# One second mix over the first two tiles, and the first sums split between VectorE and Pool

## The chip, the cores and the metric

The kernel runs on one core of a Trainium2 chip. The metric is the device time of one execution in microseconds (us); before the change it is 791.39 us, the median of three runs (790.71 to 791.91).

## The reference

Three stages follow each other on two batches of 4160 positions with 192 channels. The first is a windowed sum with 8 heads, the second and third are channel mixes with 1024 hidden channels.

```python
w = softmax(weight_gen, axis=-1)                     # 8 heads x 7 positions
out = np.einsum('bshk,bskhg->bshg', w, x_unf)        # 7 positions of x, weighted and summed
# first mix
xk = mu_k * x + (1.0 - mu_k) * x_prev                # xr the same with mu_r
k = np.maximum(xk @ w_k, 0.0)
x = sigmoid(xr @ w_r) * (k * k @ w_v)
# second mix
h = np.maximum(x @ w_in, 0.0)
conv_out = sum(conv_w[k] * hp[:, k:k + S, :] for k in range(3))   # three neighbouring positions
out = h * sigmoid(conv_out) @ w_out
```

## The kernel before, in words

The positions are cut into ten tiles (`SIZES`: 256, 248, seven of 472, 352). For each tile and batch the work has these steps.

- **Sums** (`attention`): for each slot (a set of 128 positions, one per partition) a `token` multiplies the 7 rows by the weights (`prod`, 1344 columns) and folds them in three additions (576, 384 and 192 columns) into `tok`. There are 2 slots in each of the first two tiles, 4 in the others. All sums are done by Pool, with one scratch tile `prod`.
- **Mixing in** (`mixing`): TensorE turns `tok` into channel-major form in a `pa` bank (matmuls with `ident`); u = 0 holds the first 128 channels of batch 0, u = 1 those of batch 1, and u = 2 the last 64 of both. ScalarE and VectorE form the mixed inputs. They are split into a high and a low part (`xA`, and for u = 2 `rm` and `mk`, which DMAs copy into `xB`).
- **First mix** (`moe1`, `gate_r`, `mix_out`): 8 groups per tile and batch. Each has five matmuls into `pa`, Relu, Square and a copy on ScalarE, a subtraction on VectorE (high and low part `s`), and five matmuls into `am` and `ar`. Two gates of five matmuls each complete it, and `mix_out` writes the result to `x2`.
- **Second mix** (`moe2`, `store`): again 8 groups per tile and batch: five matmuls into `pc`, four operations on ScalarE and four on VectorE (`h`, the taps, Sigmoid, `g`), and five matmuls into `bm` and `br`. `carry` copies the last two columns of a tile in front of the next.

The weights arrive as 64-bit floats and are turned into a high and a low 32-bit part by `narrow` and `split` (VectorE, ScalarE and the tile `stage`). This goes on beside the first tiles. The softmax weights `sw` of tiles 0, 1 and 2 are made separately; those of tiles 3 to 9 are one load, worked on tile by tile.

The order on each engine is not written by hand. Each closure enters a plan with a due time (`at`), and `Program.schedule` simulates the engines with the costs of `cost` and always takes the ready operation that is due first. The result is a fixed list of instructions for each engine. An engine runs its list in order and waits where an input is missing. All instructions are therefore on line 167 in the profile.

Of the kernel before, what the change touches and what calls it, by code (L numbers as in the profile page):

```python
# [12 lines left out]
AX = mybir.AxisListType  # L13

NB, SEQ, DM, NH, KS, DFF = 2, 4160, 192, 8, 7, 1024
SIZES = [256, 248] + [472] * 7 + [352]
NTILE = len(SIZES)
STARTS = [sum(SIZES[:i]) for i in range(NTILE)]
NMAX = max(SIZES)

PART = [128] * NTILE
SLOTS = [2, 2] + [4] * 7 + [3]
# [2 lines left out]
WIN = KS * DM  # L25
NF = DFF // 128
LAG = 10


def f(ap):  # L30
# [3 lines left out]
class Program:  # L34
# [37 lines left out]
    def cost(self, eng, method, out, ins, pointer):  # L72

        n = self.count(out)
        src = [self.space(x) for x in ins]
        if method == "dma_start":
            return 0.6, 0.0
        if eng == "PE":
            busy = max(n * 0.00045 + 0.002, 0.109)
            return busy, busy + 0.24  # L80
        if eng == "ACT":
            near = bool(src) and src[0] == "PSUM"
            p = 0.1 if pointer else 0.0
            return (0.06 if near else 0.09) + p + n / 1200, (0.2 if near else 0.24) + p + n / 1200
        if eng == "DVE":
            if method == "tensor_reduce":
                n = self.count(ins[0])
            if method == "reciprocal":
                return 0.07 + n / 160, 0.2 + n / 160
            if method in ("tensor_scalar", "tensor_copy", "memset") and "PSUM" not in src:  # L90
                return 0.07 + n / 1920, 0.2 + n / 1920
            stt = method == "scalar_tensor_tensor"
            return (0.13 if stt else 0.07) + n / 960, (0.26 if stt else 0.2) + n / 960
        if eng == "POOL":
            busy = 0.1 + (n / 455 if method == "tensor_tensor" else n / 270)
            return busy, busy + 0.12
        return 0.6, 0.6

    def schedule(self):
# [41 lines left out]
        start = [0.0] * n  # L141
        for _ in range(n):
            t, eng = min((max(free[e], min(ready[i] for i in w)), e) for e, w in open_.items() if w)
            i = min((i for i in open_[eng] if ready[i] <= t), key=lambda i: (self.ops[i][4], i))
# [12 lines left out]
            if self.ops[i][1] == "dma_start":  # L157
                wires[eng] = max(wires[eng], t + dur[i] + 0.6) + moved[i]
                end = wires[eng] + 0.8
            for j in succ[i]:  # L160
                ready[j] = max(ready[j], t + dur[i] if eng == "PE" == self.ops[j][0] else end)
                left[j] -= 1
                if not left[j]:
                    open_[self.ops[j][0]].append(j)
# [17 lines left out]
def conv_moe_kernel(ctx: ExitStack, tc: tile.TileContext, xp, wg_first, wg_rest, mus, w_k, w_v, w_r, w_in, conv_w, w_out, out):  # L182
# [11 lines left out]
    def ring(name, n, shape, dtype=F32):  # L194
        return Ring([new(f"{name}{j}", shape, dtype) for j in range(n)])
# [48 lines left out]
    sm = []  # L244
# [126 lines left out]
    def softmax(j, a, b, eng, times, bank):  # L371
# [18 lines left out]

        for t, fn in zip(times, (lambda: fold(m, ALU.max), lambda: each(m, ALU.subtract), s3,
                                 lambda: fold(z, ALU.add), s5, lambda: each(m, ALU.mult))):
            at(t, fn)

# [6 lines left out]
    def attention(i, b, t_load, t, dt_, eng, hold=(0.0, 0.0)):  # L401
# [7 lines left out]
        def token(l):  # L409
            if i not in tok_t:  # L410
                tok_t[i] = tok_r()
            p = prod
            y = p.rearrange("p (k d) -> p k d", k=KS)
            w = sw[:, sum(slots[:i]) + b * L + l].unsqueeze(2).to_broadcast([128, KS, DM // NH, NH])
            eng.tensor_tensor(p.rearrange("p (k g h) -> p k g h", k=KS, h=NH),
# [159 lines left out]
    def carry(i, b, t):  # L575
        def go():
            if i == 0:
                POOL.memset(f(x2[b][:, :, 0:2]), 0.0)
            else:
                n = SIZES[i - 1]  # L580
                ACT.copy(x2[b][:, :, 0:2], f(x2[b][:, :, n:n + 2]))
            if i == NTILE - 1:
                n = SIZES[i]
                POOL.memset(f(x2[b][:, :, n + 2:n + 4]), 0.0)
        at(t, go)

    def mix_out(i, b, t):
        N = SIZES[i]
        X = x2[b]
        c = slice(2, N + 2)  # L590
        m, r = am_r.tiles[0], ar_r.tiles[0]

        def d0():
# [28 lines left out]

    def moe2(i, b, fi, t):
        last = i == NTILE - 1
        N = SIZES[i] + (2 if last else 0)
        X = x2[b]
        st = {}
        sl = slice(128 * fi, 128 * fi + 128)
# [50 lines left out]
        at(t + 2.75, go2)  # L679

    def store(i, b, t):
        N = SIZES[i]
        last = i == NTILE - 1
        a = 1 if i == 0 else 0
        n = N + (1 if last else 0)
        t0 = STARTS[i] - 1
        st = {}

        def e0():
# [22 lines left out]
    def identity():  # L712
# [12 lines left out]
    prepare((-99.75, -99.7, -99.4), [(-82, chunk_rem(w_k, wkB, True)), (-81, chunk_in(w_k, wkA, 0)),  # L725
                                     (-0.5, chunk_out(w_v, wv, 0)), (0.4, chunk_out(w_v, wv, 1)), (1.0, chunk_in(w_k, wkA, 1)),
                                     (1.4, chunk_out(w_v, wv, 2)), (2.4, chunk_out(w_v, wv, 3)), (3.4, chunk_r()),
                                     (4.4, chunk_rem(w_in, wiB, False)), (5.0, chunk_in(w_in, wiA, 0)), (6.0, chunk_out(w_out, wo, 0)),
                                     (6.4, chunk_conv()), (7.0, chunk_in(w_in, wiA, 1)), (8.0, chunk_out(w_out, wo, 1)),
                                     (9.0, chunk_out(w_out, wo, 2)), (10.0, chunk_out(w_out, wo, 3))])  # L730
    softmax_load(2, wg_rest[:, slots[1] * KH:(slots[1] + slots[2]) * KH], -99.3)
    softmax(2, 0, slots[2], POOL, (0.9, 0.91, 0.92, 0.93, 0.94, 0.95), None)
    softmax_load(3, wg_rest[:, (slots[1] + slots[2]) * KH:], 10.2, 40.0)
# [7 lines left out]
    for i in range(NTILE):  # L741
# [6 lines left out]
        for b in range(NB):  # L748
            t = T + 8 * b
            carry(i, b, t + 7)  # L750
            for k in range(2):
                gate_r(i, b, k, t + 5.12 + k)
            for fi in range(NF):
                moe1(i, b, fi, t + fi)
                moe2(i, b, fi, t + fi + LAG)
            mix_out(i, b, t + 8.52)
            store(i, b, t + LAG + 10.02)

    for t, _, fn, hold in sorted(plan, key=lambda e: e[:2]):
        prog.now, prog.hold = t, hold  # L760
# [66 lines left out]
```

## Time and profile before

| what | value |
|---|---|
| median of three runs | 791.39 us (790.71 to 791.91) |
| the profiled execution | 793.36 us, its span 791.6 us |
| TensorE busy | 697.2 us (88%), 3505 matmuls |
| ScalarE busy | 666.5 us (84%), 1441 instructions |
| VectorE busy | 631.4 us (80%), 1137 instructions |
| Pool busy | 506.2 us (64%), 368 instructions |
| mean granted TensorE clock | 0.973 |

The span is what the profiler records on the core; 1.8 us of the execution lie around it. The page divides the span into 40 slices. TensorE is idle in the first two, at 50 to 70% in the next five, at 90% or more from the eighth to the thirty-eighth, and lower in the last two. Pool is busy from the start to about 430 us.

### The profile page before, as it was taken

To read this page: it belongs to the slowest core of one execution; us is meant where nothing else is said; L and a number is where in the kernel's file an instruction comes from. 1 tells how busy PE (TensorE), PEld (TensorE's weight loads), DVE (VectorE), ACT (ScalarE), POOL (GpSimd) and SP (SyncE) were. 2 spreads that over 40 slices of the span, in tenths; PEclk is the share of its full clock that TensorE was granted. 3 is DMA by queue.
4 is the path that set the end of the run, shared out by engine and by line. 5 is a ranking of instruction groups with operands and counts; after the bars stand their busy time and mean duration, and the time that the engine had idled before them with its cause. 6 is when DMAs were issued, how large, how long until landed. Compare 5 with 4: busy or idle time off the path is not lost.

```text
span 791.6 us, 10781 instructions
## 1 busy us (share of the span) xinstructions
PE 697.2 (88%) x3505; PEld 607.3 (77%) x3505; DVE 631.4 (80%) x1137; ACT 666.5 (84%) x1441; POOL 506.2 (64%) x368
## 2 busy tenths in 40 slices
PE   0066776999999999999999999999999999999964
PEld 0054675898888888888888888888888888889843
DVE  5987977887878787878877887879787878788764
ACT  2467798998989899989898989989898989899854
POOL 5898888899999999999999789295401101000000
PEclk9997786999999999999999999999999999999998
DMA  7685010130130112112121211020002000100000
GB/s 202 194 277 174 13 51 11 58 103 10 61 99 19 51 69 59 59 51 91 28 69 51 68 46 58 7 68 1 20 12 56 20 1 21 35 19 1 20 14 14
DMA packets 19241, 45.09 MB, mean 57 GB/s; under 512 B 3057, under 2 KB 14705, under 8 KB 19057
## 3 DMA queue, kind: packets, MB, share of 16 engines
q1 hardware_dynamic: 19184, 44.41, 18.9%
q8 instruction: 27, 0.44, 0.2%
q14 instruction: 30, 0.24, 0.1%
HBM read 27.40 MB, written 6.39 MB: 43 GB/s over the span
## 4 chain that ended last, share of the span: by engine, by line
PE 68%; ACT 15%; DVE 13%; issue 2%; DMA 2%; SPq 0%; ACTq 0%; DVEq 0%
PE pa L167 21%; PE pc L167 16%; PE am L167 10%; PE bm L167 9%; PE ar L167 7%; PE br L167 5%; DVE pc L167 4%; ACT pa L167 2%; ACT pc L167 2%; DVE stage L167 2%; ACT h L167 2%; ACT g L167 2%; ACT L167 1%; DMA stage<-in_moe_w_k_dram 1%; DVE bm L167 1%
## 5 line engine op out<-in xcount | busy, mean ns | idle before, releaser
L167 DVE SCALAR_TENSOR_TENSOR pc<-h,cw,pc 128x472 f32<-128x472 f32 (+3 forms) x320 | 208.1, 650 | 39.5 <-ACT pc L167 36.7
L167 POOL TENSOR_TENSOR prod<-rows,sw 128x1344 f32<-128x1344 f32 x70 | 216.1, 3087 | 12.8 <-DMA rows<-in_x_dram 7.8
L167 ACT ACTIVATE pa<-pa 128x472 f32<-128x472 f32 (+3 forms) x320 | 160.8, 505 | 39.1 <-PE pa L167 35.2
L167 POOL TENSOR_TENSOR prod<-prod 128x576 f32<-128x576 f32 (+1 forms) x140 | 171.0, 1221 | 8.6
L167 PE MATMUL bm<-g,wo 128*128 128x472 f32 (+3 forms) x480 | 148.7, 360 | 21.3 <-ACT g L167 21.1
L167 PE MATMUL am<-s,wv 128*128 128x472 f32 (+3 forms) x480 | 147.0, 367 | 7.1 <-ACT s L167 5.8
L167 DVE TENSOR_TENSOR pc<-h,pc 128x472 f32<-128x472 f32 (+3 forms) x160 | 94.7, 592 | 59.2 <-ACT pc L167 57.9
L167 PE MATMUL pa<-xA,wkA 128*128 128x472 f32 (+3 forms) x480 | 125.9, 368 | 7.5 <-DVE s L167 3.4
L167 PE MATMUL pc<-x,wiA 128*128 128x474 f32 (+3 forms) x480 | 121.6, 361 | 3.5 <-DVE g L167 3.5
L167 POOL TENSOR_TENSOR xA<-mk,xA 128x472 fp32r<-128x472 f32 (+2 forms) x36 | 40.4, 1128 | 123.1 <-ACT xA L167 96.6
L167 PE MATMUL ar<-s,wv 128*128 128x472 f32 (+3 forms) x320 | 112.6, 364 | 4.9 <-DVE x L167 3.3
L167 PEld LDWEIGHTS bm<-g,wo 128*128 128x128 f32 x480 | 88.3, 191 | 35.4 <-ACT g L167 26.0
L167 PE MATMUL br<-g,wo 128*128 128x472 f32 (+3 forms) x320 | 112.4, 355 | 1.4 <-DVE ob L167 1.4
L167 DVE TENSOR_TENSOR s<-pa,s 128x472 fp32r<-128x472 f32 (+3 forms) x160 | 93.7, 586 | 16.8 <-ACT s L167 15.8
L167 DVE TENSOR_TENSOR g<-pc,g 128x472 fp32r<-128x472 f32 (+3 forms) x160 | 93.8, 586 | 15.5 <-ACT g L167 14.0
L167 PEld LDWEIGHTS am<-s,wv 128*128 128x128 f32 x480 | 89.1, 197 | 21.4 <-ACT s L167 11.0
L167 PEld LDWEIGHTS pa<-xA,wkA 128*128 128x128 f32 x480 | 87.6, 199 | 19.9 <-DVE s L167 6.4
L167 ACT ACTIVATE pc<-h,cw 128x472 f32<-128x472 f32 (+3 forms) x160 | 99.7, 623 | 1.8
L167 PEld LDWEIGHTS pc<-x,wiA 128*128 128x128 f32 x480 | 85.7, 193 | 15.9 <-DVE g L167 5.8
L167 ACT ACTIVATE h<-pc 128x474 f32<-128x474 f32 (+3 forms) x160 | 84.4, 527 | 11.4 <-PE pc L167 8.3
L167 ACT ACTIVATE pc<-pc 128x472 f32<-128x472 f32 (+3 forms) x160 | 80.9, 506 | 14.0 <-DVE pc L167 13.0
L167 PE MATMUL pa<-xB,wkB 128*128 128x472 f32 (+3 forms) x320 | 89.8, 362 | 1.5 <-DMA xB<-mk 1.5
(105 smaller groups left out, 1066.4 us busy)
## 6 DMA issues: line engine op xcount, KB each, us to landing
rows<-in_x_dram SPq DMA_DIRECT2D x14, 960.0 KB, 4.5
xB<-rm SPq DMA_DIRECT2D x28, 118.0 KB, 2.3
xB<-mk SPq DMA_DIRECT2D x28, 118.0 KB, 2.3
out_dram<-om SPq DMA_DIRECT2D x14, 236.0 KB, 2.0
rows<-in_x_dram SPq DMA_DIRECT2D x4, 768.0 KB, 7.1
rows<-in_x_dram SPq DMA_DIRECT2D x2, 864.0 KB, 4.5
out_dram<-ob SPq DMA_DIRECT2D x14, 118.0 KB, 2.2
stage<-in_moe_w_v_dram SPq DMA_DIRECT2D x4, 384.0 KB, 3.9
```

Source lines behind the costliest of these rows:

```text
L167: getattr(self.real[eng], method)(*a, **k)
```

## The change

- The second tile gets 220 positions instead of 248, and the seven large ones 476 instead of 472.
- The second mix of tile 0 is no longer run by itself. Its input stays in `x2` in front of that of tile 1 (`OFFSET`), and one second mix of 476 columns (`UNIT`) follows once tile 1 has gone through the first mix. `carry`, `moe2` and `store` work on these units.
- VectorE does the sums of batch 0 of tile 0 with a scratch tile of its own (`prod0`, which lies in the second `tok` buffer). Pool does those of batch 1, with a hold of 16 us in the planner. The rows of tile 0 are loaded before the softmax weights.
- The softmax of tiles 3 to 9 takes its Exp as one instruction of 3024 columns. Its other steps, and the preparation of `w_in`, `w_out` and `conv_w`, have later due times.
- The planner knows other costs for Pool, and lets an engine wait up to 0.2 us for an operation that is due before -80.

```diff
-SIZES = [256, 248] + [472] * 7 + [352]
+SIZES = [256, 220] + [476] * 7 + [352]
+OFFSET = [0, SIZES[0]] + [0] * (NTILE - 2)
+UNIT = [None, SIZES[0] + SIZES[1]] + SIZES[2:]
+AHEAD = 0.2
...
-            busy = 0.1 + (n / 455 if method == "tensor_tensor" else n / 270)
-            return busy, busy + 0.12
+            busy = 0.15 + (n / 455 if method == "tensor_tensor" else n / 270)
+            return busy, busy + 0.1
...
+    prod0 = tok_r.tiles[1].rearrange("p a b -> p (a b)")[:, :WIN]
...
-            p = prod
+            p = prod0 if eng is DVE else prod
...
-    at(-100.5, consts)
+    at(-99.8, consts)
...
-    attention(0, 0, -99.9, -90, 0.1, POOL)
-    attention(0, 1, -99.6, -83.7, 0.1, POOL)
+    attention(0, 0, -100.1, -90, 0.1, DVE)
+    attention(0, 1, -99.6, -83.7, 0.1, POOL, (0.0, 16.0))
...
-        softmax(3, a, b, POOL, (16.5 + 0.3 * j, 16.6 + 0.3 * j, 19.5 + 0.1 * j, 20.5 + 0.5 * j, 20.6 + 0.5 * j, 24.9 + 16 * j), None)
+        softmax(3, a, b, POOL, (22 + 0.4 * j, 25 + 0.02 * j, None, 26.5 + 0.7 * j, 26.6 + 0.7 * j, 28.9 + 16 * j), None)
+    at(26, lambda: ACT.activation(sm[3][0], sm[3][0], ACTF.Exp))
...
-                moe2(i, b, fi, t + fi + LAG)
+                if i:
+                    moe2(i, b, fi, t + fi + LAG)
             mix_out(i, b, t + 8.52)
-            store(i, b, t + LAG + 10.02)
+            if i:
+                store(i, b, t + LAG + 10.02)
```

VectorE's list right behind the softmax of tile 0, before (the operations on `bm`, `pc0` and `stage` turn the weights `w_k` into 32-bit parts):

```order
L167 TENSOR_TENSOR sw_107<-sw_107,smz0_108 128x224
L167 TENSOR_SCALAR bm_117<-bm_117 128x512
L167 SCALAR_TENSOR_TENSOR bm_117<-stage_75,bm_117 128x512
L167 TENSOR_SCALAR pc0_113<-bm_117 128x512
L167 SCALAR_TENSOR_TENSOR stage_75<-stage_75,pc0_113 128x512
```

The same place now:

```order
L173 TENSOR_TENSOR sw_107<-sw_107,smz0_108 128x224
L173 TENSOR_TENSOR tok1_80<-rows0_76,sw_107 128x1344
L173 TENSOR_TENSOR tok1_80<-tok1_80 128x576
L173 TENSOR_TENSOR tok1_80<-tok1_80 128x384
L173 TENSOR_TENSOR tok0_79<-tok1_80 128x192
```

The four operations of a sum, twice, stand in front of the weights now (the second four read alike).

Pool's list where the sums of tile 1 begin (`rows0` again, into `tok1`), before:

```order
L167 TENSOR_TENSOR tok0_79<-prod_78 128x192
L167 TENSOR_TENSOR prod_78<-rows0_76,sw_107 128x1344
L167 MEMSET att0_81 128x1
L167 MEMSET att1_82 128x1
L167 TENSOR_TENSOR prod_78<-prod_78 128x576
```

The same place now:

```order
L173 TENSOR_TENSOR sw_107<-sw_107,smz2_110 128x448
L173 TENSOR_TENSOR sw_107<-sw_107,smz1_109 128x224
L173 MEMSET att0_81 128x1
L173 MEMSET att1_82 128x1
L173 TENSOR_TENSOR prod_78<-rows0_76,sw_107 128x1344
L173 TENSOR_TENSOR prod_78<-prod_78 128x576
```

The two small fills of `att` for u = 1 of tile 0 stood behind the first multiplication of tile 1, and stand ahead of it now.

ScalarE's list at the first Exp of tiles 3 to 9, before:

```order
L167 ACTIVATE pa0_111<-pa0_111 128x256 x2
L167 ACT_TABLE_LOAD
L167 ACTIVATE sw_107<-sw_107 128x448
L167 ACT_TABLE_LOAD
L167 ACTIVATE pc0_113<-pc0_113 128x256
```

The same place now:

```order
L173 ACTIVATE pa1_112<-pa1_112 128x220 x2
L173 ACT_TABLE_LOAD
L173 ACTIVATE sw_107<-sw_107 128x3024
L173 CAST rm00_85<-mk0_83 128x476
L173 ACT_TABLE_LOAD
```

Six further Exps with their table loads are gone, and the copy to `rm00` (tile 2, u = 2) stands behind the one that is left.

Pool's list ahead of this Exp, now (it ends the sums of tile 2, then subtracts the maxima of tiles 3 to 9):

```order
L173 TENSOR_TENSOR tok0_79<-prod_78 128x192
L173 TENSOR_TENSOR sw_107<-sw_107,stage_75 128x448 x6
L173 TENSOR_TENSOR sw_107<-sw_107,stage_75 128x336
L173 TENSOR_TENSOR xA00_87<-mk0_83,xA00_87 128x476
L173 TENSOR_TENSOR xA10_89<-mk1_84,xA10_89 128x476
```

The seven subtractions are behind all eight sums of tile 2 now, where six of them stood between the sums before.

## Rows read from the trace of the kernel before

**Rows 1.** By stretch: PE, PEld, DVE, ACT, POOL busy; granted clock, DMA share, GB/s.
```profile
20.00:40.00 20.00, 1.76 (x5) 0.76 (x5) 19.64 (x43) 8.07 (x20) 17.89 (x17) 1.00 0.69 194
40.00:140.00 100.00, 68.75 (x372) 61.57 (x372) 81.81 (x182) 77.65 (x195) 87.76 (x68) 0.81 0.32 103
140.00:160.00 20.00, 17.88 (x145) 16.85 (x143) 17.20 (x44) 19.12 (x59) 17.89 (x14) 1.00 0.17 60
160.00:200.00 40.00, 39.70 (x255) 36.23 (x256) 30.24 (x69) 35.92 (x96) 38.45 (x26) 1.00 0.19 55
```

**Rows 2.** Waits of 0 to 42 us: total, times, longest.
```profile
PE pa L167 <- POOL tok L167: 37.8, 4, 15.4
```

**Rows 3.** Timeline of Pool around 40 us: start, length, operation.
```profile
38.75 0.59 POOL L167 TENSOR_TENSOR tok<-prod 128x192 f32<-128x192 f32 x1
39.42 3.02 POOL L167 TENSOR_TENSOR prod<-rows,sw 128x1344 f32<-128x1344 f32 x1
...
45.75 3.04 POOL L167 TENSOR_TENSOR prod<-rows,sw 128x1344 f32<-128x1344 f32 x1
```

**Rows 4.** Chain that ended last, near 261 us: start, length, ten matmuls of 472 columns.
```profile
261.21 2.14 PE pa L167 x10
```

**Rows 5.** Busy groups by shape, ScalarE: total us, mean ns, idle before.
```profile
L167 ACT ACT_TABLE_LOAD x14 | 18.0, 1283 | 5.2 <-DMA sw<-in_first_dram 5.0
L167 ACT ACTIVATE sw<-sw 128x448 f32<-128x448 f32 x7 | 4.0, 578 | 0.2
```

**Rows 6.** Busy groups by shape, VectorE.
```profile
L167 DVE SCALAR_TENSOR_TENSOR pc<-h,cw,pc 128x472 f32<-128x472 f32 x224 | 158.8, 709 | 28.3 <-ACT pc L167 26.1
L167 DVE SCALAR_TENSOR_TENSOR pc<-h,cw,pc 128x256 f32<-128x256 f32 x32 | 15.4, 480 | 2.3 <-ACT pc L167 2.2
L167 DVE TENSOR_REDUCE stage<-sw 128x64 f32<-128x448 f32 x12 | 11.5, 977 | 5.5 <-ACT sw L167 5.5
L167 DVE RECIPROCAL stage<-stage 128x64 f32<-128x64 f32 x6 | 3.3, 550 | 0.4
L167 DVE TENSOR_SCALAR bm<-bm 128x512 uint32<-128x512 uint32 x4 | 2.8, 691 | 4.5 <-ACT bm L167 4.5
L167 DVE TENSOR_TENSOR sw<-sw,smz 128x224 f32<-128x224 f32 x2 | 0.8, 392 | 0.1
```

**Rows 7.** DMA issues of the first 1.9 us: KB each, us to landing.
```profile
rows<-in_x_dram SPq DMA_DIRECT2D x1, 768.0 KB, 7.3
sw<-in_first_dram SPq DMA_DIRECT2D x1, 112.0 KB, 3.7
```

**Rows 8.** Timeline of the loads: start and length of two issues on SP's queue.
```profile
3.98 0.55 SPq L167 DMA_DIRECT2D rows<-in_x_dram  x1
4.57 0.48 SPq L167 DMA_DIRECT2D sw<-in_rest_dram  x1
```

**Rows 9.** DMA issues of 3.9 to 4.7 us: KB each, us to landing.
```profile
rows<-in_x_dram SPq DMA_DIRECT2D x1, 768.0 KB, 10.6
...
sw<-in_rest_dram SPq DMA_DIRECT2D x1, 112.0 KB, 10.3
```

**Rows 10.** Timeline of VectorE: first and last operation of the softmax of tile 0.
```profile
4.92 0.55 DVE L167 TENSOR_REDUCE smz<-sw 128x32 f32<-128x224 f32 x1 [2.37 <-DMA sw<-in_first_dram]
...
7.89 0.39 DVE L167 TENSOR_TENSOR sw<-sw,smz 128x224 f32<-128x224 f32 x1
```

**Rows 11.** Timelines of Pool and VectorE near 120 us: one VectorE operation, twice.
```profile
118.67 3.06 POOL L167 TENSOR_TENSOR prod<-rows,sw 128x1344 f32<-128x1344 f32 x1
120.17 1.61 DVE L167 TENSOR_SCALAR stage<-stage 128x64 f32<-128x64 f32 x1
...
126.38 0.19 DVE L167 TENSOR_SCALAR stage<-stage 128x64 f32<-128x64 f32 x1
```

**Rows 12.** Busy groups by shape, Pool.
```profile
L167 POOL TENSOR_TENSOR sw<-sw,stage 128x448 f32<-128x448 f32 x12 | 13.6, 1140 | 5.6 <-DVE stage L167 3.4 <-ACT h L167 2.2
L167 POOL TENSOR_TENSOR xA<-mk,xA 128x248 fp32r<-128x248 f32 x4 | 2.8, 721 | 4.4 <-ACT xA L167 4.4
```

More of the change, by code (lines that the diff above doesn't have):

```diff
@@ L143, in schedule @@
             t, eng = min((max(free[e], min(ready[i] for i in w)), e) for e, w in open_.items() if w)
-            i = min((i for i in open_[eng] if ready[i] <= t), key=lambda i: (self.ops[i][4], i))
+            i = min((i for i in open_[eng] if ready[i] <= t + (AHEAD if self.ops[i][4] < -80 else 0.0)), key=lambda i: (self.ops[i][4], i))
+            t = max(t, ready[i])
             open_[eng].remove(i)
@@ L160, in schedule @@
             for j in succ[i]:
-                ready[j] = max(ready[j], t + dur[i] if eng == "PE" == self.ops[j][0] else end)
+                ready[j] = max(ready[j], t + dur[i] if eng in ("PE", "POOL") and eng == self.ops[j][0] else end)
                 left[j] -= 1
@@ L392, in softmax @@
                                  lambda: fold(z, ALU.add), s5, lambda: each(m, ALU.mult))):
-            at(t, fn)
+            if t is not None:
+                at(t, fn)
     rows_t, tok_t = {}, {}
@@ L578, in go @@
                 POOL.memset(f(x2[b][:, :, 0:2]), 0.0)
-            else:
-                n = SIZES[i - 1]
+            elif i > 1:
+                n = UNIT[i - 1]
                 ACT.copy(x2[b][:, :, 0:2], f(x2[b][:, :, n:n + 2]))
@@ L589, in mix_out @@
         X = x2[b]
-        c = slice(2, N + 2)
+        c = slice(OFFSET[i] + 2, OFFSET[i] + N + 2)
         m, r = am_r.tiles[0], ar_r.tiles[0]
@@ L624, in moe2 @@
         last = i == NTILE - 1
-        N = SIZES[i] + (2 if last else 0)
+        N = UNIT[i] + (2 if last else 0)
         X = x2[b]
@@ L681, in store @@
     def store(i, b, t):
-        N = SIZES[i]
+        N = UNIT[i]
         last = i == NTILE - 1
-        a = 1 if i == 0 else 0
+        a = 1 if i == 1 else 0
         n = N + (1 if last else 0)
-        t0 = STARTS[i] - 1
+        t0 = STARTS[i] - OFFSET[i] - 1
         st = {}
@@ L727, in conv_moe_kernel @@
                                      (1.4, chunk_out(w_v, wv, 2)), (2.4, chunk_out(w_v, wv, 3)), (3.4, chunk_r()),
-                                     (4.4, chunk_rem(w_in, wiB, False)), (5.0, chunk_in(w_in, wiA, 0)), (6.0, chunk_out(w_out, wo, 0)),
-                                     (6.4, chunk_conv()), (7.0, chunk_in(w_in, wiA, 1)), (8.0, chunk_out(w_out, wo, 1)),
-                                     (9.0, chunk_out(w_out, wo, 2)), (10.0, chunk_out(w_out, wo, 3))])
+                                     (6.0, chunk_rem(w_in, wiB, False)), (8.0, chunk_in(w_in, wiA, 0)), (10.0, chunk_out(w_out, wo, 0)),
+                                     (10.4, chunk_conv()), (12.0, chunk_in(w_in, wiA, 1)), (14.0, chunk_out(w_out, wo, 1)),
+                                     (16.0, chunk_out(w_out, wo, 2)), (18.0, chunk_out(w_out, wo, 3))])
     softmax_load(2, wg_rest[:, slots[1] * KH:(slots[1] + slots[2]) * KH], -99.3)
     softmax(2, 0, slots[2], POOL, (0.9, 0.91, 0.92, 0.93, 0.94, 0.95), None)
-    softmax_load(3, wg_rest[:, (slots[1] + slots[2]) * KH:], 10.2, 40.0)
+    softmax_load(3, wg_rest[:, (slots[1] + slots[2]) * KH:], 18.2, 50.0)
     for j in range(NTILE - 3):
         a, b = (sum(slots[3:3 + k]) for k in (j, j + 1))
-        softmax(3, a, b, POOL, (16.5 + 0.3 * j, 16.6 + 0.3 * j, 19.5 + 0.1 * j, 20.5 + 0.5 * j, 20.6 + 0.5 * j, 24.9 + 16 * j), None)
+        softmax(3, a, b, POOL, (22 + 0.4 * j, 25 + 0.02 * j, None, 26.5 + 0.7 * j, 26.6 + 0.7 * j, 28.9 + 16 * j), None)
+    at(26, lambda: ACT.activation(sm[3][0], sm[3][0], ACTF.Exp))
     mixing(0, 0, -88, 0.1)
```

## The prediction

> **What bounds the kernel now.** I read the busy time by stretch first, then the waits of the start, then timelines. From 160 us on, TensorE is busy 39.70 of 40 us [rows 1]: there only the amount of matmul work counts. Before that it is starved. To 40 us it waits 37.8 us for the sums of tile 0 [rows 2], the last of which Pool starts at 38.75 [rows 3]. From 40 to 140 us it executes 372 matmuls at a mean granted clock of 0.81, ScalarE and VectorE being busy 78 and 82 of 100 us [rows 1]. So the end moves by what TensorE has done by some time after the start, compared with before, minus any work added.
>
> I measure that in us of matmul work at the full rate. Ten matmuls of 472 columns take 2.14 us [rows 4], so one takes 0.214 us and a column 0.00045 us: 256 columns 0.116, 248 columns 0.113, 476 columns 0.216. By 140 us there are 377 matmuls, 372 from 40 us on and five before [rows 1], 12 of them turns of `tok` (0.07 each, my estimate for 128 columns with its overhead); that is 365 x 0.116 + 0.8 = 43.2 us. The 145 of the next stretch add 16.3: **59.5 us of work at 160 us** is the mark to beat. The 40 us behind it hold 38.2 us of work by the same count, a rate of 0.96.
>
> **Work added and removed on TensorE.** Seven tiles of 476: 7 x 340 matmuls x 4 columns x 0.00045 = +4.3 us. Tile 1's first mix, 180 matmuls with 28 columns less: -2.3. The second mix of both tiles, 160 matmuls of about 0.216 in place of 320 of 0.116 and 0.113 (their halos counted): 34.6 against 37.0, -2.4. Together about -0.4: the matmul work does not decide.
>
> **What the merge frees.** Two taps of 256 columns took 2 x 480 ns of VectorE, one of 472 takes 709 [rows 6]: 0.25 us saved for each pair. With four operations on each of two engines in 16 groups this is some 16 us on each (an estimate that gives all operations this saving). Ten table loads of 1.283 us [rows 5] go, 12.8 us of ScalarE. All of it lies between 80 and 160 us, where these engines set the pace, but in this kernel each engine runs a fixed list, so I follow the chain instead of adding up.
>
> **Start of the sums.** Before, `sw` lands 3.7 us and the rows 7.3 us after issue [rows 7], and the softmax ends 3.4 us after `sw` (4.92 to 8.28) [rows 10]. Now the rows are issued first. If `sw` still lands at 4.9, the softmax ends at 8.3, with the rows there at 8.0; if it lands just behind the rows, as a small load behind large rows does in [rows 8, 9] (4.57 + 10.3 against 3.98 + 10.6), it lands at 8.3 and the softmax ends at 11.7. The latter row is of the same pattern, but in a busier queue; I take 10.4 and keep both ends.
>
> A sum on VectorE: 392 ns at 224 columns and 691 at 512 [rows 6] give 0.16 us plus 1.04 ns a column, so 1344, 576, 384 and 192 columns take 1.56 + 0.76 + 0.56 + 0.36, with gaps 3.35 us, and two 6.7. Alone they would end at 17.1 (15.0 to 18.4).
>
> Pool's rows land at 3.98 + 10.6 = 14.6 [rows 8, 9], in the midst of this. Does VectorE wait for Pool there? The same VectorE operation took 0.19 us once and 1.61 at 120.17, where Pool's multiplication ran from 118.67 to 121.73: it ended right behind it [rows 11]. That operation has one input from SBUF; the two-input products of the softmax ran while Pool was idle, so no row shows a sum beside Pool. The Trainium skill (SBUF — State Buffer, section SBUF: two separate sides) says that a VectorE operation with two SBUF inputs, as a sum's all are, also shares a port pair with GpSimd, and that the later one blocks until the other instruction has ended. By that rule the two engines would alternate from 14.6 on; without it the sums would not touch each other. In numbers of rows: alternating with Pool's 3.0, 1.4, 1.0 and 0.6 us, VectorE ends at S = 20 to 27.4, depending on the start; not alternating, at 15.0 to 18.4. I take S = 22.5.
>
> **From S to the second tile.** Behind the sums VectorE has 24 operations up to the inputs of u = 2: twelve of 512 columns at 0.69 [rows 6], one of 384, six of 256 at 0.42 to 0.48, three reductions, two small; 14.2 us, less some 1 us of overlap: 13.2. Pool's two fills of `att` wait for the last of them, and the multiplication of tile 1 is behind the fills. So tile 1's sums start at S + 13.4 = 35.9 (39.42 before [rows 3]); before, those fills stood behind the multiplication.
>
> **Pool to the Exp.** Four sums of tile 1 at 6.33 us each (39.42 to 45.75 [rows 3], 6.4 with later ones), and one product of 1.14: 26.6. Eight sums of tile 2: 51.2. Six subtractions for tile 1's inputs at about 0.66 [rows 12], 4.0, and 1.5 for waits on ScalarE (4.4 us before in such places [rows 12]; here VectorE is ahead). Seven subtractions of maxima, 7.7 [rows 12]. Sum: 35.9 + 26.6 + 56.7 + 7.7 = 126.9.
>
> **The Exp and behind it.** ScalarE cannot pass its Exp. 448 columns take 0.578 us [rows 5], so 3024 at most 3.9, without the fixed part about 2.8: it ends at 129.8. Then VectorE takes seven reductions (0.977), seven additions (0.19 to 1.6 beside Pool) and seven reciprocals (0.55) [rows 6, 11], with a few groups in between: some 16 us, to T = S + 123.5 = 146. From there on nothing but matmul work is left in TensorE's way. It has then done tile 0's first mix (180 x 0.116), 172 matmuls of 220 columns (0.101), 50 of the merged second mix, five of tile 2 and 20 turns: 51.8 us. By 160 us that is 51.8 + 14 x 0.96 = 65.2, against 59.5: 5.7 of work, 5.9 us of time. I add 0.4 for the work, and take off 1.5 because TensorE idled in front of the softmax's end: the clock granted to the starved stretch is 0.81 [rows 1], between 1.2 and 2.4 GHz, and 15 to 20 matmuls at the lower level cost 1.5 to 4. **Gain: 4.8 us**, and the profiled execution of 793.36 would become 788.6. Against the median of 791.39, 0.25% below it, that is 786.6; I say **787**.
>
> **The rivals.**
> - *The engines do not hinder each other, and the softmax comes early*: then Pool's own end sets the turn (14.6 + 12.7 = 27.3, u = 2 ready at 30), tile 1 starts at 30.1, T = 140, work at 160 us 71.0: 11 us gained, **781**. For it: no row shows two-input waits. Against it: the one-input wait in [rows 11].
> - *The late start*: `sw` behind the rows and strict alternation, S = 27.4, T = 151, work at 160 us 60.5; gain within 0.5 us of nothing, **791**. All else in the change is then spent on the wait. This is also how it would read if the merge only removed work from engines with slack.
> - *VectorE becomes the bound* (the slower side). From S to T its list sums to 124 us, 111 with overlaps; my T allows it 12 us of idleness, 10%. It was idle 2% of 20 to 40 us but 18% of 40 to 140 us [rows 1]. With 18% again, T = S + 135.6 = 158, work at 160 us 53.8, 6 us lost: **796**. It decides from 13.5% of idleness on, where T reaches 150.7. For it: every weight is prepared later than before, by the 6.7 us of the sums and the wait, on the same engine that feeds each group. Against it: part of the 18% stood behind the seven Exps, 5.5 us in front of the reductions alone [rows 6], and one Exp is left.
>
> **How the numbers follow.** The forecast 0.40, no hindrance 0.17, the late start 0.16, VectorE as the bound 0.27. About 0.2%, 1.6 us, is what a measurement of this kernel can tell from no change. The first two are faster by more: 0.57. The third is the same: 0.16. The last is slower: 0.27. The forecast's own range is 783 to 790 (S from 20 to 25). With the bounds of the others to either side, 779 to 797 should hold the time 8 times in 10.
>
> **What the profile will show.** Right: VectorE's sums end near 22.5 with waits on Pool between them; Pool's first multiplication of tile 1 at 36; the long Exp at 127 to 130; TensorE nearly idle before it and full from 146 on; four table loads. Wrong would be: sums without stretched operations (then 781), a softmax end past 11 us (791), or VectorE with more than 13% of idle time between 23 and 146 us (796). If TensorE is not full from 150 to 200 us, or the large tiles run at less than 0.96, the step on the rest of the kernel failed.

## The result: 799.7 us, slower by 1.3%

The changed kernel takes **799.69 us** (median of four runs, 798.63 to 805.68) against 791.65 us for the kernel before in the same session (790.71 to 792.52). The ratio is 1.0132, with a 95% interval of 1.0098 to 1.0167. The profiled execution took 799.31 us, its span is 797.5 us; 791.6 us was the span of before. The forecast was 787, faster, with a range of 779 to 797. It was wrong in sign and in size. The profiled execution of before (793.36 us) lies 1.7 us above its median and this one 0.4 us below its own, so the two profiles show 5.9 of the 8.0 us.

The page gives the changed kernel's busy time, share and count for each engine:

```profile
PE 702.1 (88%) x3345; PEld 597.6 (75%) x3345; DVE 640.1 (80%) x1079; ACT 646.9 (81%) x1355; POOL 496.3 (62%) x360
```

ScalarE lost 20 us of work and Pool 10, VectorE gained 9, TensorE executes 160 matmuls less. None of that is where the time went. The stretches of the start show it (busy time by stretch, the columns as in [rows 1]):

```profile
20.00:40.00 20.00, 3.66 (x11) 2.19 (x11) 19.61 (x36) 7.50 (x18) 11.79 (x13) 1.00 0.47 138
40.00:140.00 100.00, 71.06 (x389) 61.19 (x390) 82.27 (x169) 68.26 (x181) 84.82 (x65) 0.89 0.40 129
140.00:160.00 20.00, 15.15 (x58) 12.77 (x59) 19.80 (x35) 11.31 (x26) 18.32 (x12) 0.63 0.18 41
160.00:200.00 40.00, 39.33 (x181) 32.92 (x180) 31.68 (x52) 34.83 (x70) 35.31 (x26) 1.00 0.16 58
...
22.50:153.60 131.10, 83.47 (x427) 70.55 (x428) 112.98 (x226) 81.35 (x211) 106.42 (x84) 0.86 0.41 126
...
149.00:154.60 5.60, 5.59 (x17) 4.97 (x18) 5.60 (x9) 2.49 (x6) 5.37 (x4) 0.50 0.00 0
```

From 140 to 160 us TensorE executes 58 matmuls (145 in [rows 1]) at a granted clock of 0.63, while VectorE is busy 19.80 of 20 us. In the line of 22.50 to 153.60, VectorE has 18.1 us of idle time between the end of its sums and the end of the long softmax, 13.8%.

To count TensorE's progress I add up, from the timeline, the columns of all matmuls that ended by a time, at 0.000453 us each. The totals are 647.7 us before and 647.6 now. By 140 us it is 42.5 before and 46.6 now, by 160 us 58.4 and **56.4**, by 250 us 143.6 and 142.8, by 700 us 582.7 and **577.7**. So the change is 2.0 us behind where TensorE fills up (0.8 at 250 us), and the large tiles lose 4.2 us more by 700 us. The last 100 us add 0.9, which makes the 5.9 us between the spans.

### The profile page after: what moved, and what is told of

Same layout as the page of the kernel before. It is cut to its first block, busy times and chain, and to the rows that moved or that the text cites. A ratio compares the mean times of both kernels' runs of the same rounds, so it can differ in the third digit from the quotient of the medians.

```text
span 797.5 us, 10286 instructions
## 1 busy us (share of the span) xinstructions
PE 702.1 (88%) x3345; PEld 597.6 (75%) x3345; DVE 640.1 (80%) x1079; ACT 646.9 (81%) x1355; POOL 496.3 (62%) x360
## 4 chain that ended last, share of the span: by engine, by line
PE 56%; ACT 11%; DVE 9%; issue 1%; POOL 1%; ACTq 0%; POOLq 0%
PE pa L173 17%; PE pc L173 14%; PE am L173 8%; PE bm L173 7%; PE ar L173 6%; PE br L173 5%; DVE pc L173 4%; ACT pc L173 2%; ACT h L173 2%; ACT pa L173 2%; ACT g L173 2%; DVE g L173 1%; DVE x L173 1%; ACT x L173 1%; DVE s L173 1%
## 5 line engine op out<-in xcount | busy, mean ns | idle before, releaser
L173 DVE SCALAR_TENSOR_TENSOR pc<-h,cw,pc 128x476 f32<-128x476 f32 (+1 forms) x288 | 201.2, 699 | 46.8 <-ACT pc L173 44.3
L173 ACT ACTIVATE pa<-pa 128x476 f32<-128x476 f32 (+3 forms) x320 | 160.4, 504 | 51.7 <-PE pa L173 47.9
L173 PE MATMUL am<-s,wv 128*128 128x476 f32 (+3 forms) x480 | 150.0, 369 | 15.4 <-ACT s L173 11.7
L173 PE MATMUL bm<-g,wo 128*128 128x476 f32 (+1 forms) x432 | 142.7, 379 | 19.0 <-ACT g L173 19.0
L173 PE MATMUL pa<-xA,wkA 128*128 128x476 f32 (+3 forms) x480 | 126.1, 371 | 17.9 <-ACT rm L173 9.7
L173 PE MATMUL pc<-x,wiA 128*128 128x478 f32 (+1 forms) x432 | 117.9, 380 | 0.0
L173 PE MATMUL ar<-s,wv 128*128 128x476 f32 (+3 forms) x320 | 113.6, 368 | 3.0 <-ACT x L173 2.9
L173 PE MATMUL br<-g,wo 128*128 128x476 f32 (+1 forms) x288 | 107.8, 375 | 1.4 <-DVE ob L173 1.4
L173 DVE TENSOR_TENSOR s<-pa,s 128x476 fp32r<-128x476 f32 (+3 forms) x160 | 93.4, 584 | 16.5 <-ACT s L173 16.3
L173 DVE TENSOR_TENSOR g<-pc,g 128x476 fp32r<-128x476 f32 (+1 forms) x144 | 91.5, 635 | 11.6 <-ACT g L173 10.8
L173 ACT ACTIVATE pc<-h,cw 128x476 f32<-128x476 f32 (+1 forms) x144 | 94.8, 658 | 1.8
L173 ACT ACTIVATE h<-pc 128x478 f32<-128x478 f32 (+1 forms) x144 | 81.5, 566 | 14.3 <-PE pc L173 11.0
L173 ACT ACTIVATE pc<-pc 128x476 f32<-128x476 f32 (+1 forms) x144 | 78.4, 544 | 14.4 <-DVE pc L173 14.3
L173 PEld LDWEIGHTS pc<-x,wiA 128*128 128x128 f32 x432 | 79.0, 191 | 13.5 <-DVE g L173 2.6
```

The costliest lines, as they stand in the source:

```text
L173: getattr(self.real[eng], method)(*a, **k)
```

## The start, step by step

VectorE's two sums, in the timeline of the changed kernel (start, length, operation), and under it Pool's first operations and the first multiplication of tile 1:

```profile
8.38 1.56 DVE L173 TENSOR_TENSOR tok<-rows,sw 128x1344 f32<-128x1344 f32 x1
9.97 4.53 DVE L173 TENSOR_TENSOR tok<-tok 128x576 f32<-128x576 f32 x3
14.54 2.64 DVE L173 TENSOR_TENSOR tok<-rows,sw 128x1344 f32<-128x1344 f32 x1
17.21 5.38 DVE L173 TENSOR_TENSOR tok<-tok 128x576 f32<-128x576 f32 x3
22.52 0.55 DVE L173 TENSOR_REDUCE smz<-sw 128x32 f32<-128x224 f32 x1
22.98 0.69 DVE L173 TENSOR_SCALAR bm<-bm 128x512 uint32<-128x512 uint32 x1
```

```profile
11.28 3.01 POOL L173 TENSOR_TENSOR prod<-rows,sw 128x1344 f32<-128x1344 f32 x1 [9.86 <-DMA rows<-in_x_dram]
14.37 3.66 POOL L173 TENSOR_TENSOR prod<-prod 128x576 f32<-128x576 f32 x2
...
36.05 3.04 POOL L173 TENSOR_TENSOR prod<-rows,sw 128x1344 f32<-128x1344 f32 x1
```

The first multiplication is undisturbed, 1.56 us. From Pool's first operation on, the two engines alternate, and what takes VectorE 1.56 us (the multiplication) and 1.74 us (the three additions) alone takes 2.64, and 4.53 and 5.38. The sums end at 22.5, as forecast, and tile 1's first multiplication is at 36.05 (forecast 35.9). The planner had Pool wait to 16 us, but this hold is in the plan alone; on the chip nothing holds Pool back when its rows land at 11.2.

The long Exp on ScalarE, what Pool did before and after it, and TensorE's idle times:

```profile
133.53 1.28 ACT L173 ACT_TABLE_LOAD   x1
134.82 2.73 ACT L173 ACTIVATE sw<-sw 128x3024 f32<-128x3024 f32 x1
```

```profile
121.29 7.53 POOL L173 TENSOR_TENSOR sw<-sw,stage 128x448 f32<-128x448 f32 x7
128.77 2.38 POOL L173 TENSOR_TENSOR xA<-mk,xA 128x476 fp32r<-128x476 f32 x2
138.10 1.19 POOL L173 TENSOR_TENSOR mk<-mk,rm 128x476 fp32r<-128x476 f32 x1 [6.96 <-ACT rm L173]
```

```profile
139.75 0.98 PE L173 MATMUL pa<-xA,wrA 128*128 128x220 f32 x3 [3.24 <-ACT r L173]
149.01 0.77 PE L173 MATMUL bm<-g,wo 128*128 128x476 f32 x1 [4.41 <-ACT g L173]
```

Pool had freed the Exp at 128.82. ScalarE was still busy with groups ahead of it and came at 133.53, then loaded its table. VectorE's sums and reciprocals behind it ran to 153.65. TensorE stood still for 4.41 us until 149.01; from there it runs on without a gap to 176 us, but up to 154.6 at the lower of its two clock levels (1.2 GHz, granted 0.50: 17 matmuls in 5.6 us), and at the higher only behind that. Pool, which was to be early, stands still for 6.96 us behind a copy that is queued behind the Exp.

## Experiments

Two theories stood against each other: that the time goes at the late Exp, and that VectorE is the bound, because everything on its list comes later. Each kernel ran beside the kernel before (790.5 to 791.1 us in these sessions).

### One part undone, one part alone

**Pool sums everything again.** From the change:

```diff
-    attention(0, 0, -100.1, -90, 0.1, DVE)
-    attention(0, 1, -99.6, -83.7, 0.1, POOL, (0.0, 16.0))
+    attention(0, 0, -99.9, -90, 0.1, POOL)
+    attention(0, 1, -99.6, -83.7, 0.1, POOL)
```

> The change without its second part: Pool sums both batches of tile 0 again, and the loads stand in their old order; merged second mix, single Exp, sizes and planner as in the change. Theory 'late Exp' (the sums worked as forecast and won Pool 3.4 us; what cost the time is that ScalarE reached the long Exp 4.7 us after Pool had freed it, and all of VectorE's and Pool's work queued behind it): Pool's sums of tile 1 start at about 39.4 again, the Exp ends no earlier than now (137.6), and the time stays at 798 to 803. Rival 'VectorE is the bound' (the two sums and their waits push all 24 weight operations and everything behind them from 8.4 to 22.6 us): VectorE starts its weights 14 us earlier, the Exp ends at 128 to 132, and the time falls by 6 to 10, to 790 to 794.

Measured: **788.86 us**, ratio 0.9981 (0.9958 to 1.0004): 10.8 us less than the change, and below the rival's range too. The late Exp falls as the main cause: here it ends at 133.8, only 3.8 us earlier (the rival had 128 to 132), and TensorE stops behind it here too, for 2.6 and 6.4 us (3.2 and 4.4 in the change). The rival has the direction and not the numbers. What does move is the end of the whole softmax, VectorE's last reciprocal. Here, and in the change:

```profile
145.42 0.44 DVE L173 RECIPROCAL stage<-stage 128x48 f32<-128x48 f32 x1
```

```profile
153.21 0.43 DVE L173 RECIPROCAL stage<-stage 128x48 f32<-128x48 f32 x1
```

It ends 7.8 us earlier, at the 146 us that the prediction had for the change. Further lines of this kernel, VectorE's first weight, the end of Pool's sums of tile 0 and its first multiplication of tile 1, and the first matmul of the second mix:

```profile
9.31 0.70 DVE L173 TENSOR_SCALAR bm<-bm 128x512 uint32<-128x512 uint32 x1 [2.49 <-ACT bm L173]
```

```profile
31.52 0.59 POOL L173 TENSOR_TENSOR tok<-prod 128x192 f32<-128x192 f32 x1
...
36.02 3.04 POOL L173 TENSOR_TENSOR prod<-rows,sw 128x1344 f32<-128x1344 f32 x1
```

```profile
102.28 0.60 PE L173 MATMUL pc<-x,wiA 128*128 128x478 f32 x2
```

In the change the last two stand at 36.05 and here:

```profile
116.63 0.60 PE L173 MATMUL pc<-x,wiA 128*128 128x478 f32 x1
```

Under the new planner Pool alone ends tile 0's sums at 32.1 (39.3 before [rows 3]) and begins tile 1 at 36.02. The split wins **nothing** there (36.05). Pool ends its share of tile 0 at 25.6 in the change, but then stands still behind VectorE:

```profile
33.48 1.13 POOL L173 TENSOR_TENSOR sw<-sw,smz 128x448 f32<-128x448 f32 x1 [7.19 <-DVE smz L173]
```

What the split costs is 13.7 us on the weights (9.31 to 22.98), and the second mix begins 14.3 us later. By 140 us TensorE has 57.0 us of work done here, 46.6 in the change.

**The softmax and the weights' due times of before,** in the change:

```diff
...
-    softmax_load(3, wg_rest[:, (slots[1] + slots[2]) * KH:], 18.2, 50.0)
+    softmax_load(3, wg_rest[:, (slots[1] + slots[2]) * KH:], 10.2, 40.0)
...
-        softmax(3, a, b, POOL, (22 + 0.4 * j, 25 + 0.02 * j, None, 26.5 + 0.7 * j, 26.6 + 0.7 * j, 28.9 + 16 * j), None)
-    at(26, lambda: ACT.activation(sm[3][0], sm[3][0], ACTF.Exp))
+        softmax(3, a, b, POOL, (16.5 + 0.3 * j, 16.6 + 0.3 * j, 19.5 + 0.1 * j, 20.5 + 0.5 * j, 20.6 + 0.5 * j, 24.9 + 16 * j), None)
```

> The change without its third part: the softmax of tiles 3 to 9 with seven Exps and the due times of before, and w_in, w_out and conv_w prepared at the due times of before. Theory 'late Exp': VectorE's 16 us block of sums and reciprocals is spread again, so TensorE does not stand still from 136 to 150 us; ScalarE pays ten table loads more (12.8 us). Saved idleness of TensorE about 8 to 10 us against some 3 to 5 of table loads: 793 to 797. Rival 'VectorE is the bound': the sums on VectorE stay, so the lateness stays, and with the weights due earlier VectorE is fuller between 23 and 100 us: 799 to 804.

Measured: **812.61 us**, ratio 1.0274 (1.0248 to 1.0300). Both missed; the rival had the direction. The single Exp with the later due times is not the loss but saves 13 us where VectorE is late.

**Merge and sizes alone,** on the kernel before:

```diff
+SIZES = [256, 220] + [476] * 7 + [352]
+UNIT = [None, SIZES[0] + SIZES[1]] + SIZES[2:]
...
+                if i:
+                    moe2(i, b, fi, t + fi + LAG)
```

> Before plus the sizes and the one second mix of tiles 0 and 1, and nothing else. Theory 'late Exp': TensorE has no block of 16 us to wait for, some 16 us of ScalarE's and VectorE's work go, so at 160 us it is 2 to 5 us ahead of before; the large tiles take 76.4 us instead of 75.25 as in the change, which is 4.4 us more than their columns explain: 790 to 794. Rival 'the merge itself costs': the second mix of tile 0 is missing as filler between 80 and 120 us, TensorE is behind before at 160 us by 2 or more, and with the large tiles the time is 796 to 800.

Measured: **794.06 us**, ratio 1.0039 (1.0019 to 1.0059), the edge of the first theory. TensorE has 62.0 us of work done by 160 us (58.4 before), and loses that lead again by the end: both profiled spans are 791.6 us.

**VectorE's sums alone,** on the kernel before (the second and third lines of the diff on `attention`, with `prod0`):

> Before plus VectorE's sums of batch 0 of tile 0, and nothing else. Theory 'late Exp': the first inputs are ready at 22 and u = 2 at 36 instead of 40, Pool starts tile 1 some 3.4 us earlier, and the seven Exps are spread; the time falls by 1 to 4, to 788 to 791. Rival 'VectorE is the bound': every weight comes later (VectorE takes them up at 22.6 instead of 8.4 us), first s at about 47 instead of 50, but the groups of tile 0 then go slower; the time rises by 5 to 10, to 797 to 802.

Measured: **799.57 us**, ratio 1.0111 (1.0089 to 1.0133). As the rival said. The split costs 8.5 us without any of the other parts, with seven spread Exps. The planner put the sums between the first weights here (the first weight comes at 9.16 us), so the lateness grows on the way: the last part of w_v is ready at 53.7 us, 45.9 before. So the one part that carries the loss is found from both sides.

### Is it lateness, and how much of it?

Four or two reductions that nobody needs stand on VectorE where the change has its sums; Pool does the sums.

```diff
+    def busy():
+        x = rows_t[0, 0][:, 0:8].rearrange("p k d -> p d k")
+        for _ in range(4):
+            DVE.tensor_reduce(out=idle, in_=x, op=ALU.max, axis=AX.X)
+
+    at(-90, busy)
```

> The kernel with Pool's sums (the first experiment, 788.9 us), with four reductions over 1536 columns put on VectorE where the change has its sums. Their result is used by nobody. By the reductions of the trace (448 columns in 0.95 us) one takes some 3.1 us, so VectorE's weights start about 12.5 us later, while Pool sums all of tile 0 undisturbed. Theory 'late weights' (what costs the time in the change is only that VectorE takes up the weights 14 us later): the last part of w_v is ready at 57 to 60 instead of 46 us, and the time is 796 to 801. Rival 'the sums themselves' (the two engines block each other, and Pool's late end for tile 0 and its waits behind VectorE are what costs): with Pool undisturbed the time stays within 3 us of 788.9.

> As before it, with two such reductions: VectorE's weights start about 6.2 us later, which is what the two sums alone would take without any blocking. Theory 'late weights', if the time goes in proportion: half of the loss, 793 to 796. If Pool's sums of tile 0, which end at 32 us, cover the first part of the lateness, less: 789 to 792. Rival 'the sums themselves': 788 to 791.

Measured: **800.71 us** (ratio 1.0126, 1.0110 to 1.0143) and **797.84 us** (1.0089, 1.0074 to 1.0104). Lateness without any sum reproduces the loss. But half of it costs nearly as much, which neither expectation had. The planner makes a new order of everything for each kernel, so the next two keep the order of the first experiment, by taking the reductions as free:

```diff
+            if out.tensor.name.startswith("idle"):
+                return 0.0, 0.0
```

> As the fifth experiment (four reductions of 2.82 us on VectorE, 11.3 us, with Pool's sums), but the planner takes them as free, so every engine's list is that of the first experiment (788.9 us) with nothing but these four instructions in it. Theory 'late weights': the lateness itself costs, 796 to 801 as with the order planned anew (800.7). Rival 'the new order' (6.2 us of lateness cost 9 us and 12.5 us cost 12, out of proportion, so it is mostly the list that the planner makes for a late VectorE that is worse): 789 to 793.

> The same with two reductions (5.6 us), in the list of the first experiment. Theory 'late weights', in proportion to the ninth: 792 to 795. Rival 'the new order': 788 to 790, against 797.8 with the order planned anew.

Measured: **797.93 us** (1.0094, 1.0069 to 1.0119) and **790.87 us** (1.0015, 0.9998 to 1.0031). The four reductions, and the weight behind them, in the first of these:

```profile
7.28 11.27 DVE L175 TENSOR_REDUCE idle<-rows 128x192 f32<-128x1536 f32 x4 [0.26 <-DMA rows<-in_x_dram]
18.46 0.69 DVE L175 TENSOR_SCALAR bm<-bm 128x512 uint32<-128x512 uint32 x1
```

The first weight comes at 18.46 and, with two reductions, at 12.22, against 9.31 without (VectorE waited 2.49 us for its input there, so the first 2 to 3 us of reductions were free). **9.2 us of lateness cost 9.1 us, and 2.9 us cost 2.0**: roughly a microsecond for a microsecond, in one and the same order. At about the same lateness the order that the planner made for it (12.39, 797.84 us) is 7 us worse than this one. The theory holds for the first kernel; the second lies between the two expectations.

But this lateness is not that of the weights alone. With four reductions Pool, too, waits for VectorE before it begins tile 1:

```profile
44.41 0.66 POOL L175 TENSOR_TENSOR sw<-sw,smz 128x224 f32<-128x224 f32 x1 [9.94 <-DVE smz L175]
...
45.15 3.04 POOL L175 TENSOR_TENSOR prod<-rows,sw 128x1344 f32<-128x1344 f32 x1
```

Tile 1's sums come 9.1 us later than in the first experiment (2.9 us with two reductions), and in the change they do not (36.05). So the price is that of all that hangs on VectorE in this order, and no run shows it for the order of the change. What the order holds fixed shows at VectorE's last reciprocal. It ends at 145.86, 147.71 and 154.17 us in the three kernels of this order, and TensorE has done 57.3 us of work by then in each; in the change it is at 153.65, with 50.5 us done.

**Pool waits for VectorE,** in the order of the change, with one more instruction on Pool:

```diff
+            if eng == "POOL" and method == "tensor_tensor" and self.first:
+                self.first()
...
+    prog.first = lambda: nc.gpsimd.tensor_tensor(prod[:, 0:1], prod0[:, 0:1], prod0[:, 0:1], op=ALU.add)
```

> The change itself, every engine's list unchanged, with one instruction more on Pool ahead of its first multiplication: it reads one column of VectorE's scratch tile, and so waits until VectorE's last sum is all but done. The planner had put Pool there anyway (at 16 us), but on the chip its rows landed at 11.2 and nothing held it. VectorE's sums should now take 6.7 us without a break and end at 15 instead of 22.5; Pool's end at 27.8 instead of 25.6. Theory 'late weights': VectorE is 7 us late instead of 14, and by the runs with the frozen list (5.6 us cost 2, 11.3 us cost 9) the time falls to 791 to 794. Rival 'the sums on VectorE cost by themselves': 797 to 800.

Measured: **797.66 us**, ratio 1.0087 (1.0066 to 1.0108), within the rival's range. The sums did run undisturbed:

```profile
8.50 1.56 DVE L176 TENSOR_TENSOR tok<-rows,sw 128x1344 f32<-128x1344 f32 x1
10.09 1.74 DVE L176 TENSOR_TENSOR tok<-tok 128x576 f32<-128x576 f32 x3
11.87 1.56 DVE L176 TENSOR_TENSOR tok<-rows,sw 128x1344 f32<-128x1344 f32 x1
13.46 1.75 DVE L176 TENSOR_TENSOR tok<-tok 128x576 f32<-128x576 f32 x3
...
55.66 0.28 DVE L176 TENSOR_TENSOR wv<-bm,wv 128x128 fp32r<-128x128 f32 x1
```

They take 6.7 us instead of 14.1, and the weights start at 15.59, 7.4 us earlier. Only some 2 us of that reach the end (the intervals of the two ratios touch). The last part of w_v is ready at 55.94 here, but at 48.92 in the kernel with two frozen reductions, though its first weight is only 3.4 us earlier. Pool is not the reason: it begins tile 1 at 31.13 here, 4.9 us earlier than in the first experiment. TensorE has done 50.7 us of work at VectorE's last reciprocal (150.96), as in the change and 6.6 less than in the order of the first experiment. So the order of the change itself, made for a VectorE that is late, is the other part of the loss. Which of its rows costs it was not separated.

**Without the maxima, with VectorE's sums** (the kernel of the next section, with the split):

> The eleventh kernel (779.2; no maxima for tiles 3 to 9, the long Exp early, old sizes) with the change's sums on VectorE. Theory 'late weights' through the first mix of tile 0 itself: still 8 to 10 us, 786 to 790. Rival 'through the long Exp': the Exp is at 67 us and nothing queues behind it, so the split costs little: 779 to 782.

Measured: **798.58 us**, ratio 1.0096 (1.0079 to 1.0113), 19.4 us above its twin without the split and above both ranges. The cost does not come through the long Exp, which ends at 74 us here; the last part of w_out is ready at 113.9 us (95.0 in the twin) and the second mix begins at 130.4 (111.2).

### The large tiles and the planner

**The sizes alone,** on the kernel before:

```diff
+SIZES = [256, 220] + [476] * 7 + [352]
```

> Before with the sizes alone: the second tile of 220 positions, seven of 476. Theory 'large tiles': a tile of 476 takes 76.4 us in every kernel that has them and one of 472 takes 75.25; of the 1.15 us the columns explain 0.61 to 0.68. Six tiles lose 2.8 to 3.2 us that the smaller second tile does not give back: 793 to 796. Rival 'the merge sets the pace' (the extra 0.5 us for a tile comes with the merged second mix and its order, not with the size): the tile takes 75.9 us and the time is 791 to 792.5.

Measured: **799.21 us**, ratio 1.0115 (1.0095 to 1.0136), above both. The period of a large tile, from one output of batch 0 to the next on SP's queue, before, and with the sizes alone:

```profile
253.64 0.35 SPq L167 DMA_DIRECT2D out_dram<-om  x1
...
479.54 0.34 SPq L167 DMA_DIRECT2D out_dram<-om  x1
...
554.74 0.35 SPq L167 DMA_DIRECT2D out_dram<-om  x1
...
629.99 0.34 SPq L167 DMA_DIRECT2D out_dram<-om  x1
```

```profile
252.04 0.35 SPq L167 DMA_DIRECT2D out_dram<-om  x1
...
481.45 0.35 SPq L167 DMA_DIRECT2D out_dram<-om  x1
...
557.86 0.35 SPq L167 DMA_DIRECT2D out_dram<-om  x1
...
634.32 0.34 SPq L167 DMA_DIRECT2D out_dram<-om  x1
```

75.2 us became 76.4, in the change as here. So the extra is the size and not the merge, which wins 5 us against this kernel (794.06). Of the 1.2 us, 340 matmuls with 2.0 ns more from start to start (0.2142 to 0.2162 us, mean over matmuls of one width behind each other) explain 0.7; what lengthens the rest was not separated. The 28 positions that left tile 1 took 4.3 us of matmul work with them (340 matmuls, 28 columns less), but the output of the first large tile (first lines) is only 1.6 us earlier for it. From there to the last output the profiled execution loses 8.1 us, which makes the 6.5 us between the two spans (791.6 and 798.1). The positions moved from a stretch where TensorE waits to one where it is full.

**The old sizes** in the first experiment (the merged second mix has 504 columns):

```diff
+SIZES = [256, 248] + [472] * 7 + [352]
```

> The kernel with Pool's sums and merged second mix, with the old sizes: 248 for the second tile, 472 for the seven large ones, so that the merged second mix has 504 columns. Theory 'large tiles': the large tiles take 75.25 us again and 3 us come back: 785 to 787. Rival 'the merge sets the pace': each tile stays 0.5 us above what its columns explain, and the time is 788 to 790.

Measured: **790.84 us**, ratio 1.0004 (0.9993 to 1.0015): no gain over the first experiment, and above both ranges. Its large tiles take 75.2 us again, but two of them take 79.9 and 78.3. Pool's sums are the reason: nine tenths of the chain that ended last from 330 to 400 us are Pool's here, and TensorE waits 5.9 us for `mk`, which stands behind Pool's operations. The changed kernel has a shorter stop of the same kind (one tile of 78.0 us). These are lines of its chain:

```profile
364.75 0.12 PE pa L173
...
364.93 3.09 POOL prod L173
368.01 1.18 POOL xA L173
369.19 1.39 POOL prod L173
370.58 1.17 POOL xA L173
...
371.78 0.72 DVE mk L173
```

**The planner's part undone,** on the first experiment:

```diff
+            busy = 0.1 + (n / 455 if method == "tensor_tensor" else n / 270)
...
+            i = min((i for i in open_[eng] if ready[i] <= t), key=lambda i: (self.ops[i][4], i))
```

> The kernel of the first experiment (Pool's sums, merged mix, single Exp, new sizes; 788.9) with the planner's old costs and without the wait ahead. Theory: with the new planner Pool's four sums of tile 0 end at 32.1 us without a break, with the old one other products stand between them and they end at 36.9 to 39.3; the first inputs of u = 1 come 5 us later, of which TensorE feels some: 790 to 794. Rival 'the planner's part is nothing': 788 to 789.5.

Measured: **790.72 us**, ratio 1.0006 (0.9993 to 1.0018), within the theory's range, though its interval touches that of the first experiment; Pool's sums of tile 0 end at 38.2 instead of 32.1.

### A version that beats both

With Pool's sums, the merged mix, the old sizes, and no maxima in the softmax of tiles 3 to 9:

```diff
+        softmax(3, a, b, POOL, (None, None, None, 26.5 + 0.7 * j, 26.6 + 0.7 * j, 28.9 + 16 * j), None)
```

> The kernel with Pool's sums, merged second mix and old sizes (790.8), without the maxima of tiles 3 to 9: seven reductions on VectorE (7 us) and seven subtractions on Pool (7.5 us) are left out, and Exp takes the weights as they are (the quotient is the same). Theory 'Pool is the next bound' (TensorE was 10 us ahead of before at 160 us there, and lost it at the fifth and sixth large tile, of which two took 79.9 and 78.3 us instead of 75.25 because Pool's sums came late): Pool is 7.5 us earlier, those two tiles take 75.3 to 76 us, and the time is 781 to 785. Rival 'TensorE's lead is lost elsewhere': 787 to 790.

Measured: **779.17 us**, ratio 0.9870 (0.9848 to 0.9892), better than expected. The Exp and the stretch of 140 to 160 us:

```profile
66.88 2.72 ACT L173 ACTIVATE sw<-sw 128x3024 f32<-128x3024 f32 x1
```

```profile
140.00:160.00 20.00, 19.95 (x92) 16.37 (x91) 16.94 (x28) 19.40 (x40) 18.20 (x15) 1.00 0.20 70
```

The Exp stands 65 us earlier, since it no longer waits for Pool, and TensorE is full from 140 us on with 76.1 us of work done by 160 (68.7 with the maxima). The fifth tile still takes 78.5 us. Of the 11.1 us between the two profiled spans 7.4 are there by 160 us, so most of the gain came with the early Exp and not, as the theory had it, with Pool's relief at those tiles. Without maxima a weight that is too large for Exp would overflow; this version holds only for inputs like these.

**No maxima at all,** on the same kernel (tiles 1 and 2 likewise):

```diff
+    softmax(0, 0, slots[0], DVE, (None, None, -94.8, -94.7, -94.6, -94.5), am_r.tiles[0])
...
```

> The eleventh kernel (779.2) with the maxima of tiles 0 to 2 left out as well: three more kinds of reductions and products, 0.95 us less for VectorE ahead of the first weights of the sums, 3.2 us of reductions and 3.6 us of Pool's subtractions less before 47 us (the quotient is the same). If Pool's sums of tile 0 set the start, they end 0.9 to 1 us earlier and tile 1's 2 to 3 us: 776 to 778.5. Rival (the start has slack, TensorE's time is set from 80 us on): 778.5 to 780.

Measured: **778.14 us**, ratio 0.9843 (0.9818 to 0.9868). It can't be told from the version before.

## Why the prediction was wrong

- **The start of the sums: the mechanism right, the number by luck.** "I take S = 22.5": 22.5. The alternation was there; VectorE's sums lasted 14.1 us instead of 6.7. But two errors cancelled: the softmax ended at 8.35 and not 10.4, and Pool's rows were there at 11.2 and not 14.6, so the sums began 2 us earlier and met Pool 3.3 us sooner.
- **To the second tile, right in time, wrong in what it is worth.** "Tile 1's sums start at S + 13.4 = 35.9": 36.05. But Pool alone, under the new planner, starts them at 36.02. I measured the split against the 39.42 us of before. That execution was late by its loads (Pool's first multiplication at 9.14 us); the kernel with the sizes alone, which has the planner and the sums of before, begins at 6.89 and starts tile 1's sums at 36.40. So there was nothing for the split to win.
- **Pool to the Exp, nearly.** 126.9 was forecast, 128.8 measured.
- **The Exp and behind it: the step that failed.** "It ends at 129.8": 137.5. I let the Exp follow Pool. ScalarE reached it 4.7 us after Pool had freed it, and its table load of 1.28 us was left out of this chain. The block behind it took 16.1 us (16 forecast), so T, the end of the long softmax, is 153.65 and not 146. TensorE's work there was about as counted (50.5 us, 51.8 forecast), so by 160 us it is 2.0 us behind before (58.4 by its columns, 59.5 by the prediction's count) and not 5.7 ahead: 7.7 of the 10.7 us between the forecast gain of 4.8 and the 5.9 lost. The kernel without the split does reach T at 145.86. The lateness of what follows the sums on VectorE stood in the prediction only among the points for the fourth rival, without a price. In the order of the first experiment it costs about a microsecond for a microsecond; how the loss of the change divides between the lateness and the new order is open.
- **The rivals.** "VectorE becomes the bound", 796 with a chance of 0.27, had the direction and the place. Put as it put it, VectorE's list was right (113.0 us busy, 111 forecast), and it was idle for 18.1 us and not 12, 13.8%, just past the 13.5% from which it decides. But this share does not tell a fast kernel from a slow one: VectorE is idle for 16.1% of 22.5 to 153.6 us in before, and for 14.8% from the first weight to the last reciprocal in the first experiment, which is faster. VectorE costs by coming late and not by being full. What brought the time past 797 is the next point.
- **The rest of the kernel, mis-sized.** The work of the matmuls is the same, as forecast (-0.1 us against -0.4), but a large tile costs 1.2 us more and not 0.61, and one of them waits 1.6 us for Pool. From 250 to 700 us this makes the 4.2 us that the prediction took as nothing, and the end adds 0.9. The smaller second tile, which was to pay for this, gave back 1.6 us where it was tried alone.

## What to carry to other kernels

Work that moves from a late engine to one that prepares inputs for everybody is paid in what that engine does next: ask which of its later results gates the bound, and price each microsecond of their lateness, before counting what the relieved engine gains. Compare a part of a change with the kernel that has all the other parts, not with one profile of the kernel before: here the kernel without the split starts the second tile's sums at the same time. Columns that leave a starved stretch for a full one are a loss, however even the total.

## What the runs showed of the hardware

VectorE's additions and multiplications with two inputs from SBUF stretch beside Pool's by up to a factor of three (5.38 us for three additions that take 1.74 alone), and Pool's stretch too (3.66 for two that take 2.47). The Trainium skill (SBUF — State Buffer, section SBUF: two separate sides) has this as an exclusive lock that is held for a whole instruction; the runs agree.

The reductions do not stretch. One over 224 columns took 0.54 us at 5.32, with Pool idle, and 0.55 at 22.52 beside Pool's additions; the four long ones took 11.27 us beside a busy Pool, 2.82 us each. The Trainium skill (SBUF — State Buffer, section Who interferes with whom) says that `tensor_reduce` never contends on this chip; the runs agree.

One input is not enough to be free of Pool: the short addition of the softmax, which takes 0.18 us at 139.31, ended right behind Pool's multiplications at 143.22 and 149.57 (3.05 us each):

```profile
144.61 1.71 DVE L173 TENSOR_SCALAR stage<-stage 128x64 f32<-128x64 f32 x1
...
150.22 2.46 DVE L173 TENSOR_SCALAR stage<-stage 128x48 f32<-128x48 f32 x1
```
